# A fused attention, gated-MLP and channel-mixing kernel: the last network's weights as scaled float16 pairs, rebuilt under the attention heads

## The chip, the cores and the metric

The kernel runs on one core of a Trainium2 chip. TensorE does the matrix products, VectorE and ScalarE work element by element, GpSimd does the causal masking and some normalizing, and SyncE's queue issues nearly all DMAs. The metric is the device time of one execution in microseconds (us), the median of three runs.

## The reference

Four sequences of 576 tokens, eight heads of 64. Causal attention with a decay is followed by two networks over 512 features. Weights of both networks come as float64.

```python
# attention, per head
scores = (q @ k.T) / 8 + cum[:, None] - cum[None, :]     # cum: running sum of log f
attn   = softmax(causal(scores))
x      = concat_heads(attn @ v)                          # (4, 576, 512)

# first network (gated, mixes tokens)
h    = relu(x @ w_in)                                    # 512 -> 1024
u, v = h[..., :512], h[..., 512:]
v_s  = w_spatial @ layernorm(v) + b_spatial
x    = (u * v_s) @ w_out                                 # 512 -> 512

# second network ("the last network")
xk = mu_k * x + (1 - mu_k) * x_prev                      # x_prev: the token before
xr = mu_r * x + (1 - mu_r) * x_prev
k  = relu(xk @ w_k)                                      # 512 -> 1024
out = sigmoid(xr @ w_r) * ((k * k) @ w_v)
```

## The kernel before

A precise product is made of two halves: an operand is kept as a high part and the remainder (a pair), and each product is three matmuls, high x high, high x low, low x high (`T3`). In the attention and the first network the pairs are float16, scaled by a power of two that is worked out from the sum of squares. In the last network (w_out and all behind it) they are float32r, without a scale.

*Order.* `body` collects steps with `add(time, priority, function)`; the time is in heads (head g has its scores transposed at time g). `run` emits them in order of time. A list scheduler then plays the whole program against modelled durations and writes each engine's order; an instruction that went through `pin` keeps its place in its engine's order. Each engine works through its list strictly in order, SyncE's DMA queue too.

*Attention.* Per head: `score` and `rowmax` (VectorE takes the row maxima), `mrow`, `scoreT`, whose `Exp` (L339) is ScalarE's, four instructions for each head, `causal` on GpSimd (L344), `pv`, `head` (copies the head out, L365, and issues its small DMA, L368). v is in two buffers, v0 for batches 0 and 2, v1 for 1 and 3; q and k wait in `nat`.

*First network.* `plan_mlp` lays the matmuls of `m1v` (L512), `m1u` (L566) and `m2` (L583) of batch b under the heads of batch b + 1. Batch 3 has no heads behind it. `m1u` is evicted by ScalarE into u, `m2` by VectorE, which multiplies u in place (L586); both have two PSUM buffers (`psm`). The result goes to DRAM (`gd`).

*Last network's weights.* `weights2` rebuilds 24 blocks of 128 x 512 from float64: w_out 4, w_k 8, w_r 4, w_v 8. Of each, `raw_load` fetches 512 KB into one of two buffers, `raw_convert` makes float32 (ScalarE L97, VectorE L100, L104, L105; the first ScalarE and the first VectorE instruction are pinned), `split` makes the pair (ScalarE L61, VectorE L62). `body` calls it after the last head (time 33.45), a block every 0.22 of a head between the rest of batch 3's first network, and goes on with the last network when that is done.

*Last network.* 2304 tokens in four chunks of 512 and one of 256. `m3` loads the gated values, splits them and multiplies by w_out; `mix` makes xk and xr with mu; `chunk` runs `m4` (w_k, relu, square, split), `m5` (w_v) two steps behind it, and `m6` (w_r, sigmoid). All of their matmuls are issued on one line, in `mm` (L722). For the next chunk `m3` and `mix` are dealt in between.

Of the kernel before, what the change touches and what calls it, by code (L numbers as in the profile page):

```python
# [39 lines left out]
class K:  # L40
# [19 lines left out]
    def split(self, src, hi, lo):  # L60
        self.nc.scalar.copy(hi, src)  # L61
        self.nc.vector.tensor_tensor(lo, src, f32(hi), ALU.subtract)  # L62
# [46 lines left out]
    def setup(self):  # L109
        nc, a, S = self.nc, self.a, self.S  # L110
        c = self.c = self.pool("const", side="left")
        self.w = self.pool("weights1", side="left")
        self.acts = self.pool("acts1", side="left")
        at = self.at = self.pool("attn", side="right")
# [11 lines left out]
        self.nat = {(nm, i): at.tile([128, 2, 5, 64], F32, name=f"{nm}nat{i}") for nm in "kq" for i in range(3)}  # L126
# [14 lines left out]
        self.junka = at.tile([128, 640], BF16, name="junka")  # L141
# [3 lines left out]
        self.v = [at.tile([128, 5, 4, 192], F32, name=f"v{i}") for i in range(2)]  # L145
# [13 lines left out]
        g.affine_select(out=self.ident, in_=self.ident, pattern=[[-1, 128]], compare_op=ALU.not_equal, fill=1.0, base=0, channel_multiplier=1)  # L159
        self.eps = c.tile([128, 1], F32, name="eps")  # L160
# [290 lines left out]
    def weights_spatial(self):  # L451
        nc, a, w, S, sw = self.nc, self.a, self.w, self.S, self.sw
        self.stp.release()
        stp = self.pool("wstage1", side="left")
        am = stp.tile([128, 8], F32, name="am")
        ws = stp.tile([128, 5, S], F32, name="ws")
        wb = stp.tile([128, 5, 1], F32, name="wb")
# [35 lines left out]
        stp.release()  # L493
# [167 lines left out]
    def weights2(self, p, names, stage, pin=False):  # L661
# [14 lines left out]
        st = {}  # L676
# [203 lines left out]
```

## Time and profile before

| what | value |
|---|---|
| median of three runs | 740.44 us (739.67 to 742.71) |
| the profiled execution | 738.6 us, of which 736.9 us are the span from the first to the last instruction |
| mean granted TensorE clock | 0.986 of 2.4 GHz |
| busy: TensorE matmuls | 668.1 us (91%) |
| VectorE, ScalarE, GpSimd | 421.1, 372.0, 180.4 us (57%, 50%, 24%) |
| DMA | 69.8 MB, 37.8% of 16 engines' time on SyncE's queue |

Busy time of TensorE is modelled: every matmul counts with its full length, though the next one starts before its end. How densely it is fed is read from the distance between starts. The granted clock is the share of 2.4 GHz that the chip gave TensorE in a stretch; it is 1.2 or 2.4 GHz at any one time.

### The profile page before, as it was taken

Reading aid. Unit: us, or ns where it says so; the run is one execution under the profiler, and the core shown is the slowest. Engines: PE = TensorE matmul, PEld = TensorE weight load, DVE = VectorE, ACT = ScalarE, POOL = GpSimd, SP = SyncE. Lnnn points to the kernel's source line nnn. Section 1 sums busy time; section 2 is a strip of 40 time slices with the busy share of each in tenths; the row PEclk is TensorE's granted clock in tenths of the full one; section 3 lists DMA queues with packets and bytes.
Section 4 is the critical chain, followed back from the end, with each engine's and each line's share of the span. In section 5 each row is a group of like instructions: output and inputs, shape, how many; then the busy total and the mean of one; then the engine's idle time right before and its main releaser. Section 6 shows DMA issues by size and latency. Waiting matters only on the chain.

```text
span 736.9 us, 11024 instructions
## 1 busy us (share of the span) xinstructions
PE 668.1 (91%) x3718; PEld 495.8 (67%) x3718; DVE 421.1 (57%) x1147; ACT 372.0 (50%) x740; POOL 180.4 (24%) x385
## 2 busy tenths in 40 slices
PE   0368978999999999999997599999999999999997
PEld 0235645566775677657765477888888888888896
DVE  4987885684656744554029789886225422732342
ACT  4626886576445853356417359655235323632431
POOL 7023635554445444444322000000000000000000
PEclk9999979999999999999999899999999999999999
DMA  8997867676664333400035464531010100010010
GB/s 218 205 200 159 190 140 148 132 157 104 137 144 106 70 65 97 105 18 18 18 113 198 130 191 143 153 106 57 1 37 7 58 0 15 17 40 1 1 58 28
DMA packets 130681, 69.78 MB, mean 95 GB/s; under 512 B 114704, under 2 KB 115312, under 8 KB 130624
## 3 DMA queue, kind: packets, MB, share of 16 engines
q1 hardware_dynamic: 128032, 67.89, 37.8%
q10 hardware_dynamic: 2592, 1.19, 0.7%
q8 instruction: 29, 0.48, 0.3%
q14 instruction: 28, 0.23, 0.1%
HBM read 42.06 MB, written 9.79 MB: 70 GB/s over the span
## 4 chain that ended last, share of the span: by engine, by line
PE 71%; DMA 11%; DVE 8%; ACT 3%; POOL 3%; issue 2%; SPq 1%; ACTq 0%; DVEq 0%; POOLq 0%
PE m L722 38%; PE o L357 10%; PE t L335 5%; PE s L302 5%; PE m L583 5%; PE m1v L512 5%; PE m1u L566 4%; DMA qA<-md 1%; POOL x L396 1%; DMA wst<-in_moe_w_k_dram 1%; DVE junk L311 1%; POOL e L344 1%; DMA sr<-rd 1%; DMA u<-in_f_dram 1%; DMA gd<-u 1%
## 5 line engine op out<-in xcount | busy, mean ns | idle before, releaser
L357 PE MATMUL o<-e,v 128*128 128x320 f32 (+4 forms) x448 | 112.6, 379 | 4.5 <-POOL e L344 2.4
L722 PE MATMUL m<-xx,moe_w_k 128*128 128x512 f32 (+1 forms) x480 | 107.5, 373 | 0.4 <-ACT x L717 0.4
L722 PE MATMUL m<-moe_w_v,k 128*128 128x512 f32 x432 | 104.8, 391 | 0.0
L311 DVE CUSTOM_DVE_ANT_0 junk<-s,mask 128x512 bf16<-128x512 f32 (+4 forms) x160 | 76.0, 475 | 47.4 <-PE s L302 41.1
L722 PEld LDWEIGHTS m<-xx,moe_w_k 128*128 128x128 f32 x480 | 83.9, 188 | 18.2 <-ACT x L717 0.9
L339 ACT ACTIVATE e<-t,qa 128x512 f32<-128x512 f32 (+1 forms) x128 | 71.7, 591 | 45.2 <-PE t L335 44.5
L722 PEld LDWEIGHTS m<-moe_w_v,k 128*128 128x128 f32 x432 | 80.7, 188 | 17.7
L357 PEld LDWEIGHTS o<-e,v 128*128 128x128 f32 x448 | 77.0, 196 | 22.1 <-POOL e L344 5.8
L344 POOL TENSOR_SCALAR_AFFINE_SELECT e<-e 128x128 f32<-128x128 f32 (+1 forms) x160 | 52.8, 346 | 114.1 <-ACT e L339 107.3
L758 DVE TENSOR_TENSOR tmp<-tmp 128x512 f32<-128x512 f32 (+1 forms) x40 | 25.5, 638 | 88.0 <-ACT tmp L757 87.8
L302 PE MATMUL s<-kT,qT 128*128 128x512 f16 (+2 forms) x192 | 56.3, 301 | 19.6 <-DVE nm L311 10.9
L583 PE MATMUL m<-wspT,vn 128*128 128x288 f16 x384 | 55.7, 294 | 2.7 <-DVE u L586 2.7
L757 ACT ACTIVATE tmp<-m 128x512 f32<-128x512 f32 (+1 forms) x40 | 22.1, 556 | 71.3 <-PE m L722 71.1
L512 PE MATMUL m1v<-win,xt 128*128 128x512 f16 x240 | 57.4, 379 | 0.7 <-POOL xt L403 0.7
L566 PE MATMUL m1u<-xt,win 128*128 128x288 f16 x384 | 52.5, 286 | 4.6 <-ACT u L568 4.6
L302 PE MATMUL s<-kA,qA 67*128 67x512 f16 (+2 forms) x192 | 51.2, 303 | 5.0 <-DMA kA<-kT 3.7
L722 PE MATMUL m<-gh,moe_w_out 128*128 128x512 f32 (+1 forms) x240 | 53.8, 373 | 1.8 <-DVE u L586 1.1
L335 PE MATMUL t<-qA,kA 69*128 69x512 f16 (+2 forms) x192 | 50.5, 289 | 5.3 <-DMA qA<-md 4.3
L396 POOL TENSOR_TENSOR x<-xo,sr 64x576 f32<-64x576 f32 x32 | 45.4, 1417 | 23.4 <-DMA sr<-rd 22.2
L708 POOL COPY x<-x 128x4 f32<-128x4 f32 x4 | 1.2, 311 | 200.9 <-ACT x L717 200.9
L722 PE MATMUL m<-moe_w_r,xx 128*128 128x512 f32 x216 | 50.3, 392 | 0.0
L335 PE MATMUL t<-qT,kT 128*128 128x512 f16 (+2 forms) x192 | 49.9, 290 | 0.0
(159 smaller groups left out, 1067.8 us busy)
## 6 DMA issues: line engine op xcount, KB each, us to landing
sr<-rd SPq DMA_DIRECT2D x32, 144.0 KB
gd<-u SPq DMA_DIRECT2D x16, 288.0 KB
out_dram<-o SPq DMA_DIRECT2D x18, 256.0 KB
knat<-in_k_dram SPq DMA_DIRECT2D x32, 128.0 KB
v<-in_v_dram SPq DMA_DIRECT2D x32, 128.0 KB
g<-gd SPq DMA_DIRECT2D x16, 256.0 KB
wst<-in_moe_w_k_dram SPq DMA_DIRECT2D x8, 512.0 KB
wst<-in_moe_w_v_dram SPq DMA_DIRECT2D x8, 512.0 KB
```

Source lines behind the costliest of these rows:

```text
L302: self.nc.tensor.matmul(s[:, o:o + n], self.tok(qn, p, h, 128 * ib - 64, 128)[0:r], self.tok(kn, p, h, k0, n)[0:r], start=(j == 0), stop=( ...
L311: self.nc.vector.tensor_tensor_reduce(out=self.junk[r0:, 0:n], in0=self.s[u % 2][r0:, o:o + n], in1=self.mask[r0:, m0:m0 + n], op0=ALU.add ...
L335: self.nc.tensor.matmul(t[:, o:o + n], self.tok(kn, p, h, 128 * c, 128)[0:r], self.tok(qn, p, h, q0, n)[0:r], start=(j == 0), stop=(j == 1))
L339: self.nc.scalar.activation(self.e[g][:, 512 * u:512 * u + n], t[:, 0:n], AF.Exp, scale=self.qa[p][:, 5:6])
L344: self.nc.gpsimd.affine_select(out=e, in_=e, pattern=[[1, n]], compare_op=ALU.is_ge, fill=0.0, base=0, channel_multiplier=-1)
L357: self.nc.tensor.matmul(o[:, 256 + f:256 + q1], v[:, c, h // 2, 64 * (h % 2):64 * (h % 2) + 128], e[:, off:off + q1 - f], start=(c == 0), ...
L396: self.held(p, self.nc.gpsimd.tensor_tensor(self.xp[r], self.xo.pop(2 * p + h)[r], self.sr[r], ALU.mult))
L512: nc.tensor.matmul(self.m1p, xt[:, xs, 128 * j:128 * j + 128], self.win[:, ws, kc, 512:1024], start=(kc == 0 and n == 0), stop=(kc == 3 an ...
L566: self.nc.tensor.matmul(o, self.win[:, ws, kc, fs], self.xt[(4 * b + kc) % 8][:, xs, ts_], start=(kc == 0 and n == 0), stop=(kc == 3 and n ...
L583: nc.tensor.matmul(o, pairs[n][0], pairs[n][1], start=(n == 0), stop=(n == 13))
L722: self.nc.tensor.matmul(out, l, r, start=(first and j == 0), stop=(last and j == len(pairs) - 1))
L758: nc.vector.tensor_tensor(tmp[:, 0:n], tmp[:, 0:n], tmp[:, 0:n], ALU.mult)
```

## The change

Four things are done together.

1. w_out, w_k and w_r become float16 pairs with a power-of-two scale for each row block (128 rows), and so do the operands that meet them: the gated values (`gh`) and xk, xr (`xx`). The scales are worked out from sums of squares (`gsq`, `gsum`, `w2_norm`, `scale3`, `scale4`) and taken out again at the evictions and in mu. w_v and k*k stay float32r.
2. The blocks of all four weights are planned like the heads' own steps (`plan_w2`): fetch, then `w2_conv`, `w2_sq`, `w2_scale`, `w2_low`, all pinned. w_out begins at time 13.9, w_k at 25.2, w_r at 31.2, w_v at 33.75 (fetch, `wv_conv`, `wv_split`).
3. To have room, the buffers of w_in and w_spatial become one area that w_out's blocks take over; v0 becomes w_k, `nat` w_k's last rows and w_r, v1 the gated values.
4. After the last head, m3(0), m3(1) and mix(0) are dealt into the first network of batch 3, a piece every 0.25 of a head. Later chunks run m3 two chunks ahead. Two of the four accumulators of m5 move to `psm`, and `m1v` of batch 3 to `ps3`.

```diff
-            nc.sync.dma_start(g[:, 0:n], self.gd[:, kc, t0:t0 + n])
-            self.split(g[:, 0:n], gh[:, 0, kc, 0:n], gh[:, 1, kc, 0:n])
+            g, s = self.g[(4 * i + kc) % 3], gm[:, 2 + kc:3 + kc]
+            if kc == 3:
+                nc.sync.dma_start(g[:, 0:n], self.gd[:, kc, t0:t0 + n])
+            nc.scalar.mul(gh[:, 0, kc, 0:n], g[:, 0:n], s)
+            nc.vector.scalar_tensor_tensor(gh[:, 1, kc, 0:n], g[:, 0:n], s, gh[:, 0, kc, 0:n], ALU.mult, ALU.subtract)
         yield
         for m in range(4):
             ps = self.ps3.tile([128, 512], F32, tag="p", bufs=4, name="m3")
-            self.mm(ps[:, 0:n], [(wo[:, ws, kc, 128 * m:128 * m + 128], gh[:, gs, kc, 0:n]) for kc in range(4) for gs, ws in T3])
-            nc.scalar.copy(x2[:, m, 1:1 + n], ps[:, 0:n])
+            self.mm(ps[:, 0:n], [(wo[kc][:, ws, 128 * m:128 * m + 128], gh[:, gs, kc, 0:n]) for kc in range(4) for gs, ws in T3])
+            nc.scalar.mul(x2[:, m, 1:1 + n], ps[:, 0:n], gm[:, 1:2])
             yield
+        self.sumsq(self.st3[:, i:i + 1], x2[:, :, 1:1 + n], gh[:, 0, :, 0:n])
...
-        xh = self.xx[w] = p.tile([128, 2, 4, 512], F32R, tag=f"xx{w}", bufs=1, name=f"xx{w}")
+        xh = self.xx[i, w] = (self.p2 if i % 2 else p).tile([128, 2, 4, 512], F16, tag=f"xx{w}", bufs=1, name=f"xx{w}")
...
+    def gsq(self, b, fc):
+        if fc == 0:
+            self.ga[b] = self.c.tile([128, 4], F32, tag="ga", bufs=2, name="ga")
+        self.pin(self.sumsq(self.ga[b][:, fc:fc + 1], self.u[:, fc], self.junka[:, 0:self.S]))
+    def gsum(self, b):
+        self.nc.vector.tensor_reduce(self.G[:, b:b + 1], self.total(self.ga[b], 4), AX.X, ALU.add)
...
+    def w2_more(self):
+        a, nc = self.a, self.nc
+        t = self.kept("v0", "w2k")
...
+        for i, nm in enumerate(("moe2_mu_k", "moe2_mu_r")):
+            nc.sync.dma_start(self.mu[:, i, 0], a[nm].rearrange("(k p) -> p k", p=128))
+        nc.vector.tensor_scalar(self.mu[:, :, 1], self.mu[:, :, 0], -1.0, 1.0, op0=ALU.mult, op1=ALU.add)
...
+    def w2_fetch(self, n):
+        nm, kc, c = self.blocks[n]
+        self.raw_load(self.raws[n % 2], nm, slice(128 * kc, 128 * kc + 128), slice(c, c + 512), self.nc.sync)
+    def w2_conv(self, n):
+        e = self.e2[n] = self.we[n % 2 if n < 4 else (n - 4) % 3]
+        self.raw_convert(self.raws[n % 2], e, True)
+    def w2_sq(self, n):
+        self.pin(self.sumsq(self.am2[:, n:n + 1], self.e2[n], self.junka[:, 0:512]))
+    def w2_scale(self, n):
...
+            self.pin(nc.scalar.mul(self.w2[nm][kc][:, 0, c:c + 512], self.e2[m], s))
+    def w2_low(self, n):
...
+            self.pin(self.nc.vector.scalar_tensor_tensor(lo, self.e2.pop(m), self.rs[:, x:x + 1], hi, ALU.mult, ALU.subtract))
...
+    def plan_w2(self):
+        add = self.add
+        add(13.0, 9, self.w2_begin)
+        add(24.45, 9, self.w2_more)
+        add(26.3, 9, self.w2_last)
+        t = [13.9 + 1.5 * i for i in range(4)] + [25.2 + 0.75 * i for i in range(8)] + [31.2 + 0.55 * i for i in range(4)]
+        for n in range(16):
+            add(13.1 if n == 0 else max(24.6 if n == 4 else 0, t[n] - 0.7), 9, self.w2_fetch, n)
+            add(t[n], 7, self.w2_conv, n)
+            add(t[n] + 0.35, 7, self.w2_sq, n)
+            if not 4 <= n < 12 or n % 2:
+                add(t[n] + 0.55, 7, self.w2_scale, n)
+                add(t[n] + 0.8, 7, self.w2_low, n)
+        for x, n in enumerate((3, 11, 15)):
+            add(t[n] + 0.9, 7, self.w2_norm, x)
+        tv = [33.75 + 0.4 * i for i in range(8)]
+        for n in range(8):
+            add(33.5 if n == 0 else tv[n - 1] + 0.02, 9, self.wv_fetch, n)
+            add(tv[n], 7, self.wv_conv, n)
+            add(tv[n] + 0.3, 7, self.wv_split, n)
...
     last = G + 1.45
-    k.run(last)
-    k.at.release()
...
-    next(w2)
-    last += 1.65
+    first = (x for y in (k.m3(0), k.m3(1), k.mix(0, 0), k.mix(0, 1)) for x in y)
     while k.steps:
-        last += 0.22
+        last += 0.25
         k.run(last)
-        next(w2, 0)
+        next(first, 0)
...
-        side = (x for y in ((k.m3(i + 1), k.mix(i + 1, 0), k.mix(i + 1, 1)) if i < 4 else ()) for x in y)
+        ys = ((k.m3(i + 2),) if i < 3 else ()) + ((k.mix(i + 1, 0), k.mix(i + 1, 1)) if i < 4 else ())
+        side = (x for y in ys for x in y)
```

## Rows read from the trace of the kernel before

**Rows 1.** Busy us by stretch: PE, PEld, DVE, ACT, POOL; clock, DMA share, GB/s.
```profile
290.00:343.00 53.00, 52.26 (x336) 34.42 (x334) 30.74 (x107) 26.07 (x52) 21.65 (x57) 1.00 0.21 49
343.00:388.50 45.50, 45.50 (x311) 31.83 (x310) 7.49 (x20) 14.62 (x30) 17.28 (x29) 1.00 0.22 67
...
388.50:431.30 42.80, 29.69 (x210) 21.42 (x208) 34.74 (x66) 22.86 (x46) 4.79 (x19) 0.92 0.52 166
431.30:458.20 26.90, 25.79 (x109) 19.92 (x109) 24.88 (x43) 22.35 (x40) 0.46 (x1) 1.00 0.53 168
458.20:736.90 278.70, 274.84 (x1260) 226.50 (x1260) 127.09 (x233) 111.78 (x205) 0.79 (x3) 1.00 0.12 38
```

**Rows 2.** TensorE in order of time, last network: start, length, line, tiles, count.
```profile
463.89 2.96 PE L722 MATMUL m<-xx,moe_w_k 128*128 128x512 f32 x12
466.69 2.96 PE L722 MATMUL m<-gh,moe_w_out 128*128 128x512 f32 x12
...
688.48 11.17 PE L722 MATMUL m<-moe_w_r,xx 128*128 128x512 f32 x48
699.49 5.65 PE L722 MATMUL m<-moe_w_v,k 128*128 128x512 f32 x24
...
716.20 1.58 PE L722 MATMUL m<-xx,moe_w_k 128*128 128x256 f32 x12
717.61 1.55 PE L722 MATMUL m<-moe_w_v,k 128*128 128x512 f32 x6
```

**Rows 3.** TensorE in order of time, first network (float16).
```profile
382.71 1.63 PE L583 MATMUL m<-wspT,vn 128*128 128x288 f16 x12
384.18 0.41 PE L583 MATMUL m<-wspT,v 128*128 128x288 f16 x2
384.42 4.26 PE L512 MATMUL m1v<-win,xt 128*128 128x512 f16 x19
388.52 3.10 PE L566 MATMUL m1u<-xt,win 128*128 128x288 f16 x24
```

**Rows 4.** TensorE by line, 388.5 to 431.2 us: busy, mean ns, idle before, releasers.
```profile
L583 PE MATMUL m<-wspT,vn 128*128 128x288 f16 x96 | 15.2, 318 | 2.7 <-DVE u L586 2.7
L566 PE MATMUL m1u<-xt,win 128*128 128x288 f16 x96 | 12.4, 286 | 4.6 <-ACT u L568 4.6
L583 PE MATMUL m<-wspT,v 128*128 128x288 f16 x16 | 3.9, 345 | 4.7 <-DVE v L553 4.7
```

**Rows 5.** ScalarE's waits, 388.5 to 431.3 us: total, times, longest.
```profile
ACT we L97 <- DMA wst<-in_moe_w_k_dram: 12.0, 4, 3.6
ACT moe_w_k L61 <- DVE we L105: 3.7, 2, 2.0
```

**Rows 6.** Steps of a block by line; L449: duration ns min/median/max.
```profile
L104 DVE SCALAR_TENSOR_TENSOR we<-we,wst 128x512 int32<-128x512 int32 x24 | 16.4, 686 | 0.8 <-ACT we L97 0.7
L97 ACT ACTIVATE we<-wst 128x512 f32<-128x512 f32 x24 | 16.2, 682 | 21.2 <-DMA wst<-in_moe_w_k_dram 12.6 <-DMA wst<-in_moe_w_v_dram 5.4 <-DVE k L62 1.8
L100 DVE TENSOR_SCALAR wst<-wst 128x512 int32<-128x512 int32 x24 | 10.2, 426 | 3.8 <-DMA wst<-in_moe_w_k_dram 1.6 <-DMA wst<-in_moe_w_v_dram 1.3 <-DMA wst<-in_moe_w_out_dram 0.7
...
L66 ACT ACTIVATE win<-wf 128x512 f16<-128x512 f32 x8 | 5.1, 633 | 5.0 <-DVE wf L105 4.9
...
L449 DVE SCALAR_TENSOR_TENSOR win<-wf,sw,win x8: 733/744/897, 34.5 to 79.7; 128x512 f16<-128x512 f32 x8
```

**Rows 7.** The exponentials (L339) by stretch: ScalarE busy (x).
```profile
0.00:290.00 290.00, 55.07 (x98) 0.98 0.68 144
290.00:343.00 53.00, 11.91 (x22) 1.00 0.21 49
```

**Rows 8.** Waits of SyncE's queue, 150 to 388 us: total, times, longest.
```profile
SPq L368 <- ACT xo L365: 43.9, 12, 9.2
```

**Rows 9.** VectorE in order of time around mu's load.
```profile
384.31 0.17 DVE L668 TENSOR_SCALAR mu<-mu 128x4 f32<-128x4 f32 x1 [4.90 <-DMA mu<-in_moe_mu_r_dram]
```

**Rows 10.** VectorE's L105 on w_in's blocks: duration ns min/median/max.
```profile
L105 DVE SCALAR_TENSOR_TENSOR wf<-wst,wf x8: 685/692/1462, 20.0 to 70.1; 128x512 int32<-128x512 int32 x8
```

More of the change, by code (lines that the diff above doesn't have):

```diff
@@ L58, in pin, with split @@
         self.tc.keep_in_program_order(ins)
[L60 to L61 removed]
+    def split(self, src, hi, lo, pin=False):
+        x = self.nc.scalar.copy(hi, src)
+        if pin:
+            self.pin(x)
         self.nc.vector.tensor_tensor(lo, src, f32(hi), ALU.subtract)
@@ L605, in plan_mlp @@
                 add(t, 6, self.m1u if k == "u" else self.m2, b, *x)
+            if k == "g" and x[1] and x[2]:
+                add(t + (0.5 if b < 3 else 0.2), 3, self.gsq, b, x[0])
+        add(s + length + (0.7 if b < 3 else 0.3), 3, self.gsum, b)
         return s + length
@@ new lines, in w2_low, with w2_norm @@
+    def w2_low(self, n):
+        nm, kc, c = self.blocks[n]
+        x = {"moe_w_out": 0, "moe2_w_k": 4, "moe2_w_r": 8}[nm] + kc
+        for m in (n - 1, n) if c else (n,):
+            c = self.blocks[m][2]
+            hi, lo = (self.w2[nm][kc][:, i, c:c + 512] for i in range(2))
+            self.pin(self.nc.vector.scalar_tensor_tensor(lo, self.e2.pop(m), self.rs[:, x:x + 1], hi, ALU.mult, ALU.subtract))
+    def w2_norm(self, x):
+        nc = self.nc
+        r = self.ri[:, 4 * x:4 * x + 4]
+        self.inv2(r, self.rs[:, 4 * x:4 * x + 4])
+        if x:
+            nc.vector.tensor_tensor(self.span[:, 1, x - 1], self.span[:, 0, x - 1], r, ALU.mult)
+            for o in range(2):
+                nc.vector.tensor_tensor(self.mu[:, x - 1, o], self.mu[:, x - 1, o], r, ALU.mult)
+            r = self.span[:, 1, x - 1]
+        nc.scalar.activation(self.junka[:, 0:4], r, AF.Square, scale=2.0 ** -25, accum_out=self.nn[:, x:x + 1])
+        self.pow2(self.nn[:, 4 + x:5 + x], self.total(self.nn[:, x:x + 1], 1), 1e-20, 15)
@@ L698, in runs, with phase3 @@
             t += m
+    def phase3(self):
+        self.ps3 = self.pool("ps3", space=PSUM)
+        self.p3 = self.pool("phase3", side="right")
+        t = self.kept("v1", "g3")
+        self.gh = t[:, 0:2048].bitcast(F16).rearrange("p (i k c) -> p i k c", i=2, k=4)
+        self.g = [t[:, 2048 + 512 * i:2560 + 512 * i] for i in range(2)] + [self.g2]
+        self.gam = t[:, 3072:3136]
+        self.chunks = [(512 * i, min(512, 2304 - 512 * i)) for i in range(5)]
+        self.x2, self.xx = {}, {}
     def m3(self, i):
```

228 lines of the change are left out of this document (139 added, 89 removed).

## The prediction

> **What bounds the kernel now.** I read the page first, then the table of busy time by stretch, then TensorE in order of time, then the list of waits. The page gives TensorE's busy share of the span (in the table above). Such a share hides idle time of less than a matmul's modelled length, so I measured spacing: from the start of one run of matmuls to the start of the next, divided by their number. The reader is to see four regimes. Up to about 180 us the attention's own latencies set the pace, and little of the change lies there. From there to 388.5 us TensorE is fed almost without a gap: 53.0 us hold 52.3 busy, the next 45.5 hold 45.5 [rows 1]. Then comes the handover, from 388.5 to 431.3 us: 29.7 busy of 42.8, at a mean granted clock of 0.92, so part of it ran at 1.2 GHz and the rest at 2.4 [rows 1]. From 431.3 us to the end it is TensorE alone: 1.1 us of idle time up to 458.2, and after that one unbroken chain of matmuls up to the last output [rows 1]. So time is won in two ways only: cheaper matmuls in the last network, and work for TensorE in the handover.
>
> **Part 1: float16 pairs.** w_out, w_k and w_r become float16 pairs, and so do the operands that they meet. Counts come from the code: four full chunks and one half chunk, three products for each pair, so m3 has 192 matmuls of 512 columns and 48 of 256, m4 has 384 and 96, m6 has 216 of 512; m5 (w_v) stays as it is. Now m4 takes 2.80 us for 12, 233.3 ns each; m3's matmuls, of the same form, are counted alike. m6 takes 11.01 us for 48: 229.4 ns. With 256 columns m4 takes 1.41 us for 12: 117.5 ns [rows 2]. Float16 with 512 columns stands in the first network: 19 in 4.10 us, 215.8 ns; with 288 columns 12 in 1.47 us, 122.5 ns [rows 3]. On the line between these two, 256 columns are 109.2 ns. The gains are 576 x 17.5 ns = 10.1 us, 216 x 13.6 ns = 2.9 us and 144 x 8.3 ns = 1.2 us: **14.2 us**. All of it lies in the stretch that TensorE sets, so it all counts. Bound below: nothing, if the weight loads of float16 tiles ran no faster here; the rows of the first network have the same shape of load, so I take the full value.
>
> **Part 2: the handover.** Between 388.5 and 431.3 us TensorE runs 96 matmuls of m1u and 112 of m2 [rows 4], at 122.5 ns each: 25.5 us of work in 42.8, so 17.3 us are lost; with the 1.1 us behind it, 18.4. The named releasers are VectorE's v (4.7), ScalarE's u (4.6) and VectorE's u (2.7) [rows 4]; the remainder is matmuls at the low clock. Behind them stands ScalarE, held in order at the first step of a block until its 512 KB have landed: 12.0 us in four waits, 3.6 the longest [rows 5]; the evictions queued behind it are late, and with two PSUM buffers TensorE is late next. All 24 blocks pass here, about 2.5 us of VectorE each (0.43 + 3 x 0.69) [rows 6], 60 us together. After the change eight blocks (w_v) are left, 20 us, and TensorE has new work that asks for none of them: m3(0) and m3(1), 96 matmuls of 215.8 ns, 20.7 us, from weights built long before. This exceeds the hole of 17.3 us. What does not go: the w_v blocks are held in the same way, with the same double-buffered 512 KB loads, the scale steps of m3 are new links (sums of u, total, four products and subtractions before each m3), and the m3 evictions are now behind held instructions too. That TensorE can be fed beside a crowded VectorE is seen at 431.3 to 458.2: VectorE busy 24.9 of 26.9, TensorE idle 1.1 [rows 1]. Left over: between 0 and the whole 17.3; I take 5, since the load falls to a third and the filler is larger than the hole. Gain **13.4 us**.
>
> **Part 3: sixteen blocks moved under the heads.** Each costs VectorE 0.43 + 0.69 + 0.69 + 0.74 = 2.55 us and ScalarE some 0.7 + 0.63 + 0.7 = 2.0 us, taking the two scalings at the rows nearest to them [rows 6]. w_out (heads 13.9 to 19) and w_r (31.2 to 33) fall where VectorE has room: it is 7.5 us busy in the 45.5 after 343 us. The eight w_k blocks are planned for heads 25.2 to 31. By 290 us 98 exponentials are done, four for each head, so head 24 is half through, and 22 more by 343 us [rows 7]: these blocks go where VectorE is busy 30.7 of 53.0 and ScalarE 26.1 [rows 1]. With 8 x 2.55 and 8 x 2.0 they come to 51.1 and 42.1: VectorE just fits, with nothing to spare. What is queued behind a held step is the row maximum of a head (VectorE) and its exponentials (ScalarE), and TensorE's score and value products wait for these. The cover is the second batch's network, which fills TensorE meanwhile, and m3 from head 33.5 on. The fetches go into SP's queue, among the heads' own DMAs; that queue is held up to 9.2 us at a time for a head's copy (12 times, 43.9 us in all, L368) [rows 8]. A fetch caught behind this lands late, and the held ScalarE step with it; each is issued 0.7 of a head, some 6 to 7 us, ahead. Bounds: 0, and 20 us if VectorE's added w_k time came through whole. The two small loads of mu move to head 24.45, behind the last product of head 23, with VectorE's steps on them: now VectorE stands 4.9 us idle for such a load [rows 9], and it may do so there. I take **3 us** for all of part 3, nearer the lower end because VectorE is nearly idle just after.
>
> One row bears on a further price. A held VectorE step of this kind usually takes 692 ns, but the longest of eight took 1462 ns while GpSimd worked [rows 10]. The Trainium skill (SBUF — State Buffer, "Who interferes with whom") says that a VectorE instruction with two SBUF inputs and a GpSimd instruction that reads SBUF lock each other out for a whole instruction; that speaks against putting 48 such steps beside the causal masks. Were each of the 48 stretched as that one was, by 0.77 us, VectorE would lose 37 us and the sum would be higher by what came through; one in eight, as the row has it, makes 4.6 us, still inside the bound above.
>
> **Part 4: small additions.** Twelve new totals on TensorE (four for u, three for the weights, five for x2), no more than a 288-column matmul each: 12 x 0.12 = 1.5 at most, I take **1 us**. Sixteen sums of squares of u and five of x2 are ScalarE's, which has room: 111.8 of 278.7 in the last stretch [rows 1]. Moving two of m5's accumulators to other banks costs nothing: the same eight banks, and three m4 groups (7.8 us) still pass between a chunk's last m5 and the next one's first; without that cover four VectorE products of 0.69, 2.8 us a chunk.
>
> **The sum.** Span 736.9 - 14.2 - 13.4 + 3 + 1 = 713.3, a gain of 23.6 us. The profiled execution took 738.6 in all, 1.7 above its span; the median of the three runs is 740.4, 1.8 above that. Taken from the median: **717**.
>
> **The rivals.**
> *The handover stays held.* The w_v steps take the place of w_k's: ScalarE waits for 512 KB eight times, TensorE still loses some 13 to 17 us. For it: the same pins, buffers and sizes. Against: a third of the blocks, and 20.7 us of filler. Price 8 to 12 us more: 725 to 729.
> *The heads thin out.* VectorE at 51 of 53 us in the w_k stretch delays the last heads, and x of the last pair, for which the last network's first stage waits. For it: no slack there, SP's waits. Against: 38 us of free VectorE right behind. With 10 to 18 us lost instead of 3: 724 to 732.
> *Both or most of the two:* the gain of part 1 is eaten by the heads and the handover gives nothing: 737 to 744, no change.
> *Slower.* One mechanism: a held step makes its engine wait for its block (DMA late behind SP's queue, or the other engine's part), and attention behind it waits along. The price decides at (14.2 + 13.4 - 1) / 16 = 1.7 us of TensorE time per block; waits of 2.0 and 3.6 us per block are what such steps cost in the handover [rows 5]. At 2.2 us a block through sixteen blocks: 35 us, so 749. Against: TensorE has a full second network as filler under the heads, which it did not have in the handover.
>
> **How the numbers follow.** The forecast, 709 to 722: 0.60. Handover still held: 0.14. Heads thinned: 0.12. No change: 0.05. Slower: 0.09. A measurement here tells about 0.5% from no change, 3.7 us. So faster 0.86, same 0.05, slower 0.09. The lower end of the range: the whole hole closed and heads untouched, 740.4 - 14.2 - 18.4 + 1 = 708.8, less 2 to 3 for the waits under the heads that may go as well: 706. The upper end takes in the held handover and most of the thinned heads: 732.
>
> **What would show it.** Part 1: 12 matmuls of m3 and m4 in 2.59 us, m6's 48 in 10.4, m5 unchanged. Part 2: m3 matmuls among those of the last m1u and m2, less than 6 us of TensorE idle time between 388 us and the first m4, the granted clock near 1.00. Part 3: TensorE's idle time from 183 to 388 us up by no more than some 3 us, VectorE above 90% at heads 25 to 31. Wrong if: TensorE waits there for VectorE's maxima or ScalarE's exponentials by more than 10 us in total, or ScalarE stands at w_v's loads while u and m3 wait for eviction, or the float16 spacing stays above 225 ns.

## The result, and the profile after

The changed kernel takes 732.53 us (median of nine runs, 730.52 to 737.62); the kernel before, run nine times beside it, 739.67. The ratio is 0.9903, 95% interval 0.9882 to 0.9924: faster by one per cent, where three were forecast. The profiled execution took 730.5 us, its span 728.8, 8.1 less than before.

Where the time went is read from the table of busy time by stretch. First the kernel after; columns as in [rows 1].

```profile
183.00:388.00 205.00, 193.80 (x1305) 134.56 (x1304) 150.08 (x466) 127.73 (x276) 89.73 (x171) 0.99 0.46 117
...
388.50:431.30 42.80, 40.39 (x230) 21.99 (x228) 28.63 (x69) 28.61 (x60) 15.08 (x29) 1.00 0.44 134
431.30:465.60 34.30, 29.53 (x203) 19.65 (x201) 25.23 (x50) 23.80 (x43) 0.19 (x1) 1.00 0.23 73
465.60:728.80 263.20, 259.40 (x1245) 157.70 (x1243) 112.26 (x247) 110.33 (x189) 0.99 (x2) 1.00 0.06 23
```

The same table of the kernel before, for the stretch under the heads:

```profile
183.00:388.00 205.00, 202.96 (x1385) 141.72 (x1383) 100.62 (x360) 99.49 (x201) 86.93 (x181) 1.00 0.36 83
```

Length less TensorE's busy time is its idle time. The handover is filled, as forecast: 42.80 - 40.39 = 2.4 us idle instead of 13.1 [rows 1], at full clock instead of 0.92. But under the heads, where the kernel before has 205.00 - 202.96 = 2.0 us, the one after has 11.2. VectorE has 49.5 us more work there and ScalarE 28.2, the DMA share is 0.46 instead of 0.36. The last head's value product starts at 377.2 us, before at 366.8. TensorE's waits there, longest first (total, times, longest):

```profile
PE t L350 <- DMA qA<-md: 4.8, 3, 2.4
PE t L350 <- ACT e L354: 1.7, 1, 1.7
PE o L372 <- POOL e L359: 1.5, 2, 1.1
PE mrow L336 <- DVE nmh L334: 1.4, 2, 0.8
...
PE s L317 <- DVE nm L326: 0.4, 1, 0.4
```

No wait stands out as the maker of nine lost microseconds: they come in pieces of 0.3 to 2.4 us, and the largest sum is the transposed scores' wait for a small DMA, the row maxima (`md`) going into qA. For VectorE's maxima (`nm`, `nmh`) and ScalarE's exponentials together TensorE waits 1.4 + 0.4 + 1.7 = 3.5 us.

The last network is read in order of time (start, length, line, tiles, count). The kernel after:

```profile
646.91 2.10 PE L890 MATMUL m<-xx,w2k 128*128 128x512 f16 x9
648.85 0.81 PE L890 MATMUL m<-xx,w2r 128*128 128x512 f16 x3
649.50 2.11 PE L890 MATMUL m<-xx,w2k 128*128 128x512 f16 x9
...
673.51 3.15 PE L890 MATMUL m<-moe_w_v,k 128*128 128x512 f32 x12
676.50 2.12 PE L890 MATMUL m<-xx,w2k 128*128 128x512 f16 x9
678.45 0.81 PE L890 MATMUL m<-xx,w2r 128*128 128x512 f16 x3
678.91 3.15 PE L890 MATMUL m<-moe_w_v,k 128*128 128x512 f32 x12
```

The kernel before, at the same place:

```profile
677.39 2.96 PE L722 MATMUL m<-xx,moe_w_k 128*128 128x512 f32 x12
680.19 2.91 PE L722 MATMUL m<-moe_w_v,k 128*128 128x512 f32 x12
682.93 2.96 PE L722 MATMUL m<-xx,moe_w_k 128*128 128x512 f32 x12
```

(w_k's last rows live in the tile w2r.) Twelve float16 matmuls by themselves take 649.50 - 646.91 = 2.59 us, as forecast. Twelve of m4 and twelve of m5 together take 678.91 - 673.51 = 5.40, before 682.93 - 677.39 = 5.54. Forecast was 2.59 + 2.74 = 5.33: of 0.21 us, 0.14 arrived. The missing 0.07 comes some 32 times (eight groups in each of four full chunks), 2.2 us. m6, now float16 too, has its 48 matmuls start at 628.22 us and the m5 behind them at 638.39: 10.2 us, where 10.4 were forecast.

### The profile page after: what moved, and what is told of

The parts are those of the page before. It is cut to its first block, busy times and chain, and to the rows that moved or that the text cites. A ratio compares the mean times of both kernels' runs of the same rounds, so it can differ in the third digit from the quotient of the medians.

```text
span 728.8 us, 11262 instructions
## 1 busy us (share of the span) xinstructions
PE 658.8 (90%) x3742; PEld 420.5 (58%) x3742; DVE 450.5 (62%) x1283; ACT 407.0 (56%) x820; POOL 193.7 (27%) x385
## 4 chain that ended last, share of the span: by engine, by line
PE 56%; DVE 13%; DMA 10%; ACT 8%; POOL 5%; issue 4%; SPq 2%; ACTq 0%; DVEq 0%; POOLq 0%
PE m L890 37%; PE o L372 6%; PE m L596 4%; PE s L317 3%; PE t L350 3%; DVE junk L326 2%; POOL x L411 2%; PE m1v L525 2%; ACT e L354 2%; PE m1u L579 2%; DVE wstage L115 1%; DVE vt L555 1%; DVE wstage L114 1%; DMA sr<-rd 1%; ACT junka L68 1%
## 5 line engine op out<-in xcount | busy, mean ns | idle before, releaser
L890 PE MATMUL m<-moe_w_v,k 128*128 128x512 f32 x432 | 112.0, 409 | 0.0
L359 POOL TENSOR_SCALAR_AFFINE_SELECT e<-e 128x128 f32<-128x128 f32 (+1 forms) x160 | 56.9, 371 | 118.4 <-ACT e L354 113.8
L890 PE MATMUL m<-xx,w2k 128*128 128x512 f16 (+1 forms) x360 | 77.4, 358 | 0.0
L930 ACT ACTIVATE tmp<-m,w2k 128x512 f32<-128x512 f32 (+1 forms) x40 | 25.8, 644 | 70.9 <-PE m L890 70.9
L596 PE MATMUL m<-wspT,vn 128*128 128x288 f16 x384 | 53.8, 288 | 3.3 <-ACT u L581 1.8
L411 POOL TENSOR_TENSOR x<-xo,sr 64x576 f32<-64x576 f32 x32 | 48.0, 1500 | 28.9 <-DMA sr<-rd 27.5
L317 PE MATMUL s<-kA,qA 67*128 67x512 f16 (+2 forms) x192 | 51.1, 304 | 4.4 <-DMA kA<-kT 3.3
L890 PEld LDWEIGHTS <-w2k 128*128 128x128 f16 x360 | 33.9, 98 | 35.0 <-issue 4.4
L890 PE MATMUL m<-g,wstage 128*128 128x512 f16 (+1 forms) x240 | 51.2, 358 | 0.0
L890 PE MATMUL m<-w2r,xx 128*128 128x512 f16 x216 | 47.5, 379 | 0.0
L579 PEld LDWEIGHTS <-win 128*128 128x128 f16 x384 | 37.1, 99 | 16.1 <-issue 6.1
```

What stands on the lines that cost most here:

```text
L317: self.nc.tensor.matmul(s[:, o:o + n], self.tok(qn, p, h, 128 * ib - 64, 128)[0:r], self.tok(kn, p, h, k0, n)[0:r], start=(j == 0), stop=( ...
L359: self.nc.gpsimd.affine_select(out=e, in_=e, pattern=[[1, n]], compare_op=ALU.is_ge, fill=0.0, base=0, channel_multiplier=-1)
L411: self.held(p, self.nc.gpsimd.tensor_tensor(self.xp[r], self.xo.pop(2 * p + h)[r], self.sr[r], ALU.mult))
L579: self.nc.tensor.matmul(o, self.win[:, ws, kc, fs], self.xt[(4 * b + kc) % 8][:, xs, ts_], start=(kc == 0 and n == 0), stop=(kc == 3 and n ...
L596: nc.tensor.matmul(o, pairs[n][0], pairs[n][1], start=(n == 0), stop=(n == 13))
L890: self.nc.tensor.matmul(out, l, r, start=(first and j == 0), stop=(last and j == len(pairs) - 1))
```

## The experiments

Each ratio is to the kernel before, run on the same chip in the same job; its median there lay between 737.8 and 741.1 us, so ratios compare better than medians. "Idle" is 192.0 us less TensorE's busy time from 183 to 375 us of the profiled execution, and "clock" is the mean granted clock of that stretch. A matmul at 1.2 GHz counts as busy all the while, so "idle" leaves out what the clock costs: 0.01 of 192 us is 1.9 us of work at 2.4 GHz. Both columns come from one execution each.

| run | median us | ratio, 95% interval | idle | clock |
|---|---|---|---|---|
| before | | 1 | 2.0 | 1.00 |
| after | 732.5 | 0.9903 (0.9882 to 0.9924) | 11.0 | 0.99 |
| e1 fetches only, long fills | 727.4 | 0.9832 (0.9791 to 0.9874) | 9.7 | 0.97 |
| e2 steps only | 725.8 | 0.9803 (0.9768 to 0.9839) | 6.3 | 0.99 |
| e4 fetches, VectorE's steps | 732.9 | 0.9893 (0.9854 to 0.9931) | 11.8 | 0.98 |
| e5 fetches, ScalarE's steps | 727.2 | 0.9826 (0.9788 to 0.9864) | 6.6 | 0.98 |
| e6 neither | 725.7 | 0.9832 (0.9802 to 0.9862) | 9.0 | 0.99 |
| e7 fetches only | 731.4 | 0.9910 (0.9880 to 0.9939) | 10.8 | 0.96 |
| e8 w_v in float16 too | 725.4 | 0.9824 (0.9790 to 0.9858) | 8.8 | 0.97 |
| e9 m1v's old banks | 739.9 | 1.0013 (0.9984 to 1.0042) | 10.6 | 0.97 |
| e10 no sums of u | 725.1 | 0.9830 (0.9796 to 0.9863) | 7.4 | 0.99 |
| e11 no blocks, no sums of u | 720.1 | 0.9754 (0.9721 to 0.9788) | 5.4 | 0.99 |
| e12 before + sums of u | 747.6 | 1.0138 (1.0106 to 1.0170) | 5.9 | 0.99 |
| e13 sums of u moved | 730.1 | 0.9868 (0.9838 to 0.9897) | 8.0 | 0.97 |
| e14 e13 and e8 | 723.2 | 0.9776 (0.9745 to 0.9806) | 8.6 | 0.99 |
| e15 e14, block steps moved | 725.2 | 0.9797 (0.9769 to 0.9825) | 11.2 | 0.98 |
| e16 e12, sums moved | 741.5 | 1.0020 (1.0002 to 1.0037) | 2.9 | 0.99 |
| e17 e11, fills late | 720.1 | 0.9757 (0.9705 to 0.9808) | 4.0 | 0.99 |
| e18 e17, mu late | 719.2 | 0.9744 (0.9708 to 0.9781) | 4.2 | 0.99 |
| e19 before, one tile | 739.8 | 1.0016 (0.9998 to 1.0034) | 2.4 | 1.00 |

**The blocks' work, taken apart.** The first theory was the prediction's own: the held steps on a full VectorE delay the heads.

```diff
 # e2_steps_only: blocks are rebuilt from a fetch buffer that was set to zero once
-            add(13.1 if n == 0 else max(24.6 if n == 4 else 0, t[n] - 0.7), 9, self.w2_fetch, n)
 # e1_fetch_only, e7_fetch_only_clean: fetched, not rebuilt
-            add(t[n], 7, self.w2_conv, n)
-            add(t[n] + 0.35, 7, self.w2_sq, n)
...
-                add(t[n] + 0.8, 7, self.w2_low, n)
 # e7 and e6_neither fill each block's place with a GpSimd memset instead; e1 with three long ones
+            add(t[n], 7, self.w2_fill, n)
 # e4_vector_steps (no ScalarE conversion or scaling; long fills)
-            self.pin(nc.scalar.mul(self.w2[nm][kc][:, 0, c:c + 512], self.e2[m], s))
+            pass
...
 # e5_scalar_steps (no VectorE conversion, scale or low part; long fills)
-        self.raw_convert(self.raws[n % 2], e, True)
+        self.pin(self.nc.scalar.mul(e, self.raws[n % 2][:, :, 1].bitcast(F32), 2.0 ** -112))
...
```

> Leaves out every held step of the sixteen blocks under the heads (conversion, sum of squares, scaling, low half); their 512 KB fetches stay, and the weight tiles of w_out, w_k and w_r hold a constant set by GpSimd. If the steps (VectorE's or ScalarE's, or the buffers that they hold) cost the heads their time: 716 to 721 us, TensorE's waits between 180 and 390 us back to about 2 us. If the fetches' traffic on the DMA engines costs it: 729 to 733, unchanged.

> The steps of the sixteen blocks stay, their fetches are left out (the two buffers are set to zero once, so the weights are zero). If the steps themselves cost the time: 729 to 733 us. If SyncE's queue (held up to 8.6 us for a buffer) or the DMA traffic costs it: 716 to 721.

> Of the sixteen blocks only VectorE's steps and the fetches stay; ScalarE's three (first conversion, sum of squares, scaling) are left out, their outputs set to zero once. If VectorE's own time in front of the row maxima is the cost: 727 to 733 us. If it is ScalarE held in order at the sum of squares until VectorE is done (13.6 us in six waits): 716 to 721.

> Of the sixteen blocks only ScalarE's three steps and the fetches stay; VectorE's are left out (scales set to one, low halves to zero). If VectorE's time or ScalarE's waits for VectorE are the cost: 716 to 722 us. If ScalarE's own 2 us for each block are the cost: 725 to 732.

> Leaves out both the fetches and the steps of the sixteen blocks under the heads; a small GpSimd fill (0.3 us, one for each block, at the block's time) gives the weight tiles a constant. What is left of the change: float16 pairs, the new order of the handover, w_v's eight blocks, the sums of u. If the sixteen blocks are all that costs the heads their time: 716 to 720 us, TensorE's loss under the heads as before the change (6 to 7 us). If the new buffers and the batch-3 products that can start only later cost part of it: 722 to 726.

> As the run with fetches only, but the weight tiles are filled by sixteen small GpSimd instructions at the blocks' times in place of three long ones, which stood in front of the causal masks. If the fetches alone cost little: within 1 us of the run with neither. If their traffic or their place in SyncE's queue delays the heads' small transfers: 3 to 6 us above it.

In the kernel after, e2, e6 and e7 the steps cost nothing and the fetches carry the price. Without fetches, e2 is as fast as e6, which has neither, though VectorE is busy 137.8 us instead of 99.3 from 183 to 375 us; with them, after and e7 differ by 0.0007. With the fetches the ratio is 0.9910 instead of 0.9832 where there are no steps (e7, e6) and 0.9903 instead of 0.9803 where there are (after, e2), 5.8 and 7.4 us more. But the fills are not as small as they were meant to be: e6's and e7's take 0.95 us each where 0.3 was expected, and twelve of the sixteen come in two rows of six under the heads.

```profile
L735 POOL MEMSET w2k<- 128x1024 f16 x6 | 5.4, 951 | 0.0
```

The other three runs speak against so plain a price. e1 and e5 fetch all blocks and are as fast as e6. e4, with the same fetches and VectorE's steps, is 5.5 us slower than e1 in the same job, as slow as the kernel after, and there TensorE does wait for VectorE's row maxima, 4.3 + 3.5 us, which is what the prediction had feared:

```profile
PE mrow L337 <- DVE nmh L335: 4.3, 4, 1.6
PE s L318 <- DVE nm L327: 3.5, 2, 3.1
```

The wait for `md` doesn't follow the fetches either. It is 1.4 us in e2, 4.8 in the kernel after and 7.5 in e7, but 0.5 in e4 and 1.1 in e1, which fetch everything, 4.9 in e5, which is fast, and 4.3 in e12 below, which fetches no block under the heads. And much of e7's loss is no wait at all but a lower clock, 0.90 from 183 to 250 us against e6's 0.97, which is 0.07 x 67 = 4.7 us. First e6, then e7:

```profile
183.00:250.00 67.00, 63.09 (x421) 43.41 (x420) 37.24 (x136) 32.60 (x71) 27.35 (x51) 0.97 0.54 121
```
```profile
183.00:250.00 67.00, 61.52 (x392) 42.23 (x392) 33.34 (x133) 29.97 (x64) 21.94 (x43) 0.90 0.81 201
```

So the price of the sixteen blocks is measured, but which part of their work makes it changes with what else GpSimd and the order hold, and the cause stays open. Two of the expectations were missed outright: e1 and e2 both fell between the two values that their theories gave.

And e6, with none of the sixteen blocks' work, still idles 9.0 us. The blocks are not the whole loss.

**The sums of u.** For the scales, ScalarE takes a sum of squares of each quarter of u (`gsq`), pinned. In the kernel after it stands like this in ScalarE's order (start, length; e is a head's exponential):

```profile
204.01 0.69 ACT L354 ACTIVATE e<-t,qa 128x512 f32<-128x512 f32 x1 [2.93 <-PE t L350]
204.60 0.67 ACT L68 ACTIVATE junka<-u 128x576 bf16<-128x576 f32 x1
205.17 0.19 ACT L68 ACTIVATION_READ_ACCUMULATOR junka<-u 128x1 f32 x1
205.27 0.68 ACT L354 ACTIVATE e<-t,qa 128x512 f32<-128x512 f32 x1
205.84 0.73 ACT L68 ACTIVATE junka<-nat 128x640 bf16<-128x640 f32 x1
```

Between two exponentials of one head 0.67 us pass from 204.60 to 205.27, in which ScalarE works for no head. It has idle time enough, 2.93 us ahead of the first, but not at this place. Theory: this step, in the middle of a head's chain, is what the heads lose. (The expectations below name the tie to VectorE's u instead; the place came up after them.) Rivals: the block steps; or an order of work that moves with any change.

```diff
 # e10_no_u_sums (after) and e11_bare_no_u_sums (e6_neither): sums of u left out, set to 1
+        g.memset(self.G, 1.0)
-                add(t + (0.5 if b < 3 else 0.2), 3, self.gsq, b, x[0])
-        add(s + length + (0.7 if b < 3 else 0.3), 3, self.gsum, b)
 # e12_before_u_sums: into the kernel before, results unused
+            if k == "g" and x[1] and x[2] and b < 2:
+                add(t + 0.5, 3, self.gsq, b, x[0])
...
```

> The kernel after, without the sums over u: the sixteen ScalarE sums of squares of u blocks and their totals are left out and the sums are set to 1 at the start, so the scales of w_r are not those of the reference; everything else is as in the kernel after. Theory U (these sums tie ScalarE to VectorE's u and so to TensorE's second products, and that delays heads): the 14 us that TensorE lost between head 14 and the last head fall to 8 or less, time 724 to 727 us, ratio about 0.98. Rival A (the held block steps themselves cost the heads): unchanged within 2 us, 731 to 734 us. Rival C (the order of work under the heads is sensitive to any change, whatever it is): a move of 2 to 8 us in either direction, with TensorE's waits at other places.

> The kernel of e6_neither (no fetches, no held steps of the sixteen blocks, plain fills in their place), also without the sums over u (set to 1). It leaves out the rebuilding of all sixteen blocks and the scales. Theory U: the 11 us that the heads still lost in e6_neither go, 714 to 720 us, ratio about 0.97. Rival A (block steps): nothing left of them here, so as e6_neither, 724 to 728 us. Rival C (order): any value between 716 and 732 us, with waits at other places than in e6_neither.

> The kernel before, with the sums over u of batches 0 and 1 added as in the kernel after (eight ScalarE sums of squares of u blocks and two totals; their results are not used). Theory U: TensorE loses 3 to 8 us more between 150 and 330 us, 743 to 748 us, ratio 1.004 to 1.011. Rival A: unchanged, 739 to 742 us, ratio within 0.003 of 1. Rival C: a move of 2 to 8 us in either direction.

That the sums cost time is shown three times; e12 lost more than expected, and e11's time lies at the upper end of its range while its idle time did not all go. With e6 they make a square: sums of u with their totals cost 0.9903 - 0.9830 = 0.0073 beside the blocks and 0.9832 - 0.9754 = 0.0078 without them, 5.4 and 5.8 us, each uncertain by some 3 us. Of e10's 5.4 us, 3.6 are idle time under the heads. Stretch from 183 to 375 us, columns as before, first the kernel after, then e10, e11 and e12:

```profile
183.00:375.00 192.00, 180.99 (x1216) 125.91 (x1215) 137.78 (x430) 119.24 (x261) 87.96 (x169) 0.99 0.45 112
```
```profile
183.00:375.00 192.00, 184.64 (x1259) 130.34 (x1258) 133.43 (x430) 119.24 (x252) 90.51 (x171) 0.99 0.46 114
```
```profile
183.00:375.00 192.00, 186.64 (x1274) 131.88 (x1273) 99.77 (x388) 97.39 (x202) 91.32 (x183) 0.99 0.34 81
```
```profile
183.00:375.00 192.00, 186.12 (x1266) 131.02 (x1265) 98.57 (x346) 99.31 (x209) 83.45 (x171) 0.99 0.34 76
```

**Place or amount.** The same eight sums of batches 0 and 1, issued behind a head's fourth exponential instead, and their two totals 0.4 of a head later; nothing is left out.

```diff
 # e13_u_sums_moved (after)
-                add(t + (0.5 if b < 3 else 0.2), 3, self.gsq, b, x[0])
-        add(s + length + (0.7 if b < 3 else 0.3), 3, self.gsum, b)
+                add(8 * b + (16.7, 16.72, 17.7, 18.7)[x[0]] if b < 2 else t + (0.5 if b < 3 else 0.2), 3, self.gsq, b, x[0])
+        add(s + length + (1.1 if b < 2 else 0.7 if b < 3 else 0.3), 3, self.gsum, b)
 # e16_before_sums_moved: e12 with the same times
 # e15_block_steps_moved: e14 with the steps of w_out and w_k behind the fourth exponential too
-        t = [13.9 + 1.5 * i for i in range(4)] + [25.2 + 0.75 * i for i in range(8)] + [31.2 + 0.55 * i for i in range(4)]
+        t = [13.68, 15.68, 16.95, 18.68, 25.68, 25.92, 26.75, 27.68, 27.95, 28.95, 29.68, 30.68] + [31.2 + 0.55 * i for i in range(4)]
...
```

> The kernel after, complete; only the eight sums of squares of u of batches 0 and 1 are issued at another time: behind a head's fourth exponential instead of between its exponentials (six of the eight move). The same instructions, the same ScalarE time. Place theory (a 0.86 us ScalarE step between the exponentials of a head delays that head, and TensorE with it): 726 to 729 us, ratio 0.982 to 0.986, as when the sums are left out (725.1). Amount theory (it is their ScalarE and buffer time, wherever they stand): 731 to 734 us, ratio about 0.99.

> e12_before_u_sums (the kernel before, with eight unused sums of squares of u) with the eight sums behind a head's fourth exponential instead of between its exponentials. Place theory: 738 to 742 us, ratio within 0.004 of 1. Amount theory: 746 to 749 us, ratio about 1.012, as e12_before_u_sums.

> e14_moved_and_v_float16 with the block steps of w_out and w_k (convert, sum of squares, scale) moved to the stretch between one head's fourth exponential and the next head's first as well. Place theory, if it holds for these steps too: 2 to 5 us less than e14_moved_and_v_float16, that is 713 to 718 us. If the block steps cost little where they are (e6_neither lost only 2.3 us less under the heads than the kernel after): within 2 us of e14_moved_and_v_float16. Rival: the steps, now bunched, wait for each other and hold the next head, 3 us or more slower than e14_moved_and_v_float16.

In the kernel before, the time of issue decides, not the amount: e16 with the very instructions of e12 is back at 1.0020, 8.7 us less, and the last head's value product starts at 368.5 us instead of 373.0 (before: 366.8). ScalarE in e16:

```profile
203.54 1.05 ACT L340 ACTIVATE e<-t,qa 128x512 f32<-128x512 f32 x2 [1.28 <-PE t L336]
204.50 0.67 ACT L66 ACTIVATE junka<-u 128x576 bf16<-128x576 f32 x1
...
205.29 0.68 ACT L66 ACTIVATE junka<-u 128x576 bf16<-128x576 f32 x1
...
207.51 0.69 ACT L340 ACTIVATE e<-t,qa 128x512 f32<-128x512 f32 x1 [1.44 <-PE t L336]
```

Both sums now lie where ScalarE waits for the next head anyway. But e12 does not pay at each link, as the theory has it. When three of its sums have run, two of them between exponentials, a head starts its exponentials at 224.93 us, before at 224.87; three heads on, one does so at 259.59, before at 254.28. e12, then the kernel before:

```profile
224.93 0.69 ACT L340 ACTIVATE e<-t,qa 128x512 f32<-128x512 f32 x1 [4.08 <-PE t L336]
...
259.59 1.27 ACT L340 ACTIVATE e<-t,qa 128x512 f32<-128x512 f32 x2
```
```profile
224.87 1.27 ACT L339 ACTIVATE e<-t,qa 128x512 f32<-128x512 f32 x2 [1.22 <-PE t L335]
...
254.28 1.26 ACT L339 ACTIVATE e<-t,qa 128x512 f32<-128x512 f32 x2
```

So those 5.3 us are lost in one place. TensorE has waited 3.1 us for `md` just ahead of it (before 1.3), and from 225 to 232 us its clock is 0.80 where the kernel before has 1.00 (e12, then before):

```profile
225.00:232.00 7.00, 7.00 (x38) 4.17 (x37) 2.25 (x12) 4.78 (x11) 1.14 (x5) 0.80 0.14 27
```
```profile
225.00:232.00 7.00, 7.00 (x43) 4.09 (x42) 6.10 (x20) 4.57 (x11) 3.08 (x11) 1.00 0.51 112
```

The four sums of the next batch, from 293 to 316 us, add nothing: e12 is 5.5 us late ahead of them (292.55 against 287.07) and 5.4 behind them (330.17 against 324.81). More is lost from 375 to 465 us, where none of the eight sums stands and the clock is 0.91 in e12, 0.94 in e16 and 0.96 before; 0.05 of 90 us is 4.5 us. First e12, then e16 and before:

```profile
375.00:465.00 90.00, 75.31 (x432) 54.10 (x431) 63.65 (x120) 47.06 (x89) 12.47 (x29) 0.91 0.47 149
```
```profile
375.00:465.00 90.00, 75.40 (x427) 54.75 (x426) 68.16 (x128) 51.70 (x98) 11.15 (x29) 0.94 0.48 156
```
```profile
375.00:465.00 90.00, 75.78 (x427) 54.73 (x426) 70.74 (x132) 52.81 (x100) 11.01 (x29) 0.96 0.50 158
```

Nor do only the sums move: around them the list scheduler writes another order. VectorE's second steps of q and k, for example, come as nq, nk in the kernel before (L270, 211.51 and 212.31 us) and as nk, nq in e12 (L271, 211.31 and 212.11). So e12 and e16 show what the time of issue is worth; whether the sums hold up the heads there or change the order of the rest isn't shown, and the third rival stands.

In the kernel after the same move gives 0.9868, halfway between the two theories' values, with an interval that reaches into both: there it isn't settled; e14, below, falls between its two values as well. Moving the block steps (e15) gained nothing; it is 0.0021 above e14, less than the intervals can tell. That agrees with steps that cost nothing where they were.

**What remains under the heads.** e11 still idles 5.4 us, 3.4 more than before.

```diff
 # e17_fills_late (e11; blocks not rebuilt, no sums of u)
-            add(t[n], 7, self.w2_fill, n)
+            add(32.9, 7, self.w2_fill, n)
...
 # e18_mu_late: e17 and
-        add(24.45, 9, self.w2_more)
+        add(32.7, 9, self.w2_more)
...
 # e19_before_one_tile: the kernel before
-        self.nat = {(nm, i): at.tile([128, 2, 5, 64], F32, name=f"{nm}nat{i}") for nm in "kq" for i in range(3)}
+        nat = at.tile([128, 3840], F32, name="nat")
...
```

> The kernel of e11_bare_no_u_sums (no rebuilding of sixteen blocks, no sums of u), with GpSimd's sixteen fills and the totals of the scales moved from the heads to behind the last head. Under the heads nothing of the change is left but the two loads of mu and the steps on them. If the fills held up the causal masks and with them the heads: the 12 us that TensorE still lost from head 14 on fall to 6 to 9 us, 713 to 718 us (beside 720.1 for e11_bare_no_u_sums). If the rest comes from elsewhere (the new buffers, or an order of work that differs by chance): 718 to 722 us.

> e17_fills_late with the two loads of mu, the VectorE steps on them and the last buffers moved behind the last head too, so that under the heads the program does what the kernel before does. If mu's load held VectorE there: 2 to 4 us less than e17_fills_late, and TensorE loses 6 to 8 us from head 14 on, as before. If not: the same as e17_fills_late within 2 us.

> The kernel before, complete; only the buffers of q and k are declared as in the kernel after (six buffers as slices of one tile of the same total size, v0 and v1 likewise as plain tiles). No instruction is added or left out. If that layout is what the heads still lose without sums and block steps (more waits between neighbouring slices, another order from the list scheduler): the last head's value product starts 3 to 6 us later than in the kernel before, 742 to 746 us, ratio 1.004 to 1.008. If not: 738 to 741 us, ratio within 0.003 of 1.

None of the three is the cause: e17 and e18 stay within 0.001 of e11's ratio, and e19's interval holds 1. In e17 and e18 the idle time is down to 4.0 and 4.2. The last value product still starts at 370.4 and 372.4 us, 3.6 and 5.6 later than before, but that is no loss under the heads: a head that starts its exponentials at 186.46 us before starts them at 189.59 and 191.18, so 3.1 and 4.7 us of it were there already.

**The last network and the handover.**

```diff
 # e8_v_float16: w_v and k*k as float16 pairs, without a scale
-            self.wv = self.p3.tile([128, 2, 8, 512], F32R, name="moe2_w_v")
+            self.wv = self.p3.tile([128, 2, 8, 512], F16, name="moe2_w_v")
...
-            t = k2[fc] = p.tile([128, 2, 512], F32R, tag="k2", bufs=4, name="k2")
+            t = k2[fc] = p.tile([128, 2, 512], F16, tag="k2", bufs=4, name="k2")
 # e9_batch3_psum
-                self.m1p = self.ps3.tile([128, 512], F32, tag="a", bufs=2, name="m1v")
+                self.m1p = self.psm.tile([128, 512], F32, tag="m", name="m1v")
 # e14_moved_and_v_float16: e13 and e8
```

> The change, with w_v and k*k as float16 pairs too (without a scale, so small values lose part of their low half). The changed kernel's m5 stands at 233 ns a matmul where it had 229. If float32r operands are what is slow: 215.8 ns for each of 432, 7.3 us less, 724 to 727 us. If m5 is slowed by something else beside it: above 225 ns, 729 or more.

> The change, but m1v of batch 3 takes the two PSUM buffers that the other batches use, so that it need not wait until the last head's buffers are given back. If the last heads lost their filler by the new buffers: TensorE's gaps of 1 to 2 us around 340 to 352 us go, 728 to 730. If VectorE's steps make these gaps: unchanged, 731 to 734.

> e13_u_sums_moved with w_v and k*k as float16 pairs too, as in e8_v_float16. If the two gains (7 us each at most) are independent, as the place theory has it: 717 to 721 us, ratio 0.970 to 0.976. Amount theory: 724 to 727 us, as e8_v_float16 alone.

e8's last network in order of time:

```profile
669.69 2.11 PE L892 MATMUL m<-xx,w2k 128*128 128x512 f16 x9
671.63 0.81 PE L892 MATMUL m<-xx,w2r 128*128 128x512 f16 x3
672.28 2.75 PE L892 MATMUL m<-moe_w_v,k 128*128 128x512 f16 x12
674.87 2.11 PE L892 MATMUL m<-xx,w2k 128*128 128x512 f16 x9
```

All 24 now take 674.87 - 669.69 = 5.18 us, 215.8 ns each. So the 0.07 us that were missing go when m5 is float16 too. What makes float32r slower there isn't shown. Alternation alone is not it: m6's 48 matmuls and the unbroken row of 24 m5 behind them take 644.17 - 628.22 = 15.95 us, where 48 at 215.8 ns and the 24 of before (643.97 - 638.49 = 5.48) make 15.84, again more. Two of m5's accumulators also stand in other banks than before, and no run moves them back. e9 shows that m1v's move out of `psm` carries the handover: with m1v back in the two buffers that u and the totals use, TensorE waits there 5.7 us at a total for ScalarE's sum behind a weight scale and 5.4 us for u, and the whole gain is gone. Its two theories, 728 to 730 and 731 to 734 us, were about the heads, and both missed the 739.9. TensorE's waits in e9 from 375 to 460 us (total, times, longest):

```profile
PE tot L73 <- ACT junka L771: 5.7, 1, 5.7
PE m1u L579 <- ACT u L581: 5.4, 5, 1.9
```

e14, complete, is the fastest whole kernel here: 0.9776 (0.9745 to 0.9806), faster than both. How much of its lead over e8 (0.9824) is the moved sums', the intervals don't tell.

## Why the prediction was right and wrong

The direction was right, the size wrong: 717 forecast, 732.5 measured, 15.5 us more.

*Part 1* was mis-sized at m5 only. The forecast left m5 unchanged; twelve of m4 and twelve of m5 take 5.40 us instead of the 5.33 that this makes. That gave back some 2.2 of the 14.2 us.

*Part 2* held in the main. From 388.5 us to just behind the start of the first m4 (448.6) TensorE is idle 7.2 us, somewhat more than the 6 that were allowed, and the clock is full:

```profile
388.50:449.00 60.50, 53.32 (x324) 31.20 (x322) 42.81 (x100) 42.66 (x84) 15.08 (x29) 1.00 0.35 108
```

The rival of a held handover did not come: ScalarE waits for w_v's blocks 3.9 us in all, against 12.0 [rows 5].

*Part 4* is the step that failed. "Sixteen sums of squares of u and five of x2 are ScalarE's, which has room: 111.8 of 278.7 in the last stretch". The room was read from the wrong stretch. Eight of the sixteen run under the heads, six of those between a head's exponentials, and a busy share says nothing of place. Priced at nothing, the sums cost 5.4 us (e10), the largest term that was missed. By what path they cost it is not shown: moving them is worth 8.7 us in the kernel before (e12, e16), but the trace of e12 loses this in one place and by the clock, not at each sum.

*Part 3* took 3 us for the sixteen blocks; with and without the sums they cost 0.9903 - 0.9832 and 0.9830 - 0.9754, 5.3 and 5.6 us. The value was too low by 2.5, the bound of 20 far too high. Its mechanism can't be seen in the kernel after: VectorE is busy 39.7 of 53.0 us in the w_k stretch, not 51.1, since only five of the eight w_k blocks start there, and its maxima and ScalarE's exponentials hold TensorE 3.5 us in all, so the sign of more than 10 us did not come, while the idle time rose by 9.2 us instead of 3. Yet e4 has just this mechanism, and no run shows which part of the blocks makes the price in the kernel after. For w_out, the room was read from a row behind 343 us; its blocks start their conversions between 163 and 229.

```profile
290.00:343.00 53.00, 50.87 (x330) 33.69 (x328) 39.66 (x121) 31.89 (x69) 22.02 (x44) 1.00 0.44 117
```

The rule of the Trainium skill that was weighed there (SBUF — State Buffer, "Who interferes with whom") agrees with the trace: the two-input steps take a mean of 965 and 843 ns under the heads, up to 1926, where [rows 6] have 686, and the eight steps of L110, L114 and L115 there that take more than 1000 ns all overlap a GpSimd instruction. Seven of these overlap its normalizing (L411, L418), which the prediction didn't count, and three are the step with one tensor input, L110. No run takes GpSimd's work away. In e2, which has these steps without fetches, they cost nothing against e6.

```profile
L114 DVE SCALAR_TENSOR_TENSOR wstage<-wstage 128x512 int32<-128x512 int32 x11 | 10.6, 965 | 4.6 <-ACT wstage L107 4.4
...
L115 DVE SCALAR_TENSOR_TENSOR wstage<-wstage 128x512 int32<-128x512 int32 x11 | 9.3, 843 | 0.2
```

The rival "the heads thin out" (724 to 732) has the place and almost the time, but its mechanism, VectorE at its limit, isn't in the profile of the kernel after; the sums of u were no part of it. "Slower" did not come: sixteen blocks at 5.5 us are 0.34 us each, far below the 1.7 at which it decides.

The account: 15.5 = 5.4 (sums of u) + 2.5 (blocks beyond 3) + 2.2 (m5) + 5.4 left open. The first two terms carry intervals of some 3 us each. Together with the 3 us that the blocks were given they make 10.9, which is already more than the 9.2 us by which the idle time under the heads grew, so it can't be said that the open part lies there. Fills, mu's load and the tile layout are excluded as its cause. The handover's 7.2 us of idle time, where 5 were allowed, may hold 2.2 of it. Another order from the list scheduler is left as a guess; it wasn't tried by itself, and e1 and e7, which differ by their fills alone and lie 0.0078 apart, show that effects of that size are possible.

## What to carry to other kernels

A step that is moved under other work isn't priced by its engine's idle share. Eight ScalarE steps of 0.67 + 0.19 us made the kernel before 1.4% slower, and the same eight at other times in the heads 0.2% (e12, e16), while 36 to 39 us more on VectorE cost nothing in one setting (e2, e6) and went with 5.5 us in another (e1, e4). Read idle shares from the stretch in which a step will run, and try it there. Test a suspected step by adding it alone to the old kernel and then moving it: this told time of issue from amount when the kernel with everything in it could not. Then look where the trace loses the time, and at the granted clock beside the idle time, before naming the path: here the loss was not at the steps.

## What was not expected of the hardware

Twelve float32r matmuls of m5 take 2.74 us in the kernel before (682.93 - 680.19), 229 ns each, where all operands around them are float32r. In the kernel after, twelve of them and twelve float16 ones take 5.40; with 2.59 for the float16 group this leaves 2.81, 234 ns each. All in float16, they take 215.8. Why the float32r ones slow down isn't shown.

The idle time of TensorE told only part of a loss. In e7 one stretch of 67 us lost 4.7 us more to a lower clock than in e6, and 1.6 more to idle time (63.09 against 61.52 us busy).
